# Four attention layers on one core: PSUM laid out by hand (3+3 score banks, one spaced background bank), small units spread singly, masks one tile late

## Chip, cores, metric

One Trainium2 chip, one core. The metric is the device time of one execution in microseconds (us), median of several. A program on one core has one span only. "Granted clock" is the share of TensorE's full clock that the throttle let through.

## The reference, cut

```python
def _A_ref(x, wqkv, wo):              # windowed: key at most 255 behind the query
    qkv = (x @ wqkv).reshape(B, S, 3, H, Dh) ...     # B 1, S 2048, D 640, H 32, Dh 20
    scores = einsum("bhqd,bhkd->bhqk", q, k) * Dh ** -0.5
    mask = (idx[:, None] - idx[None, :] >= 0) & (idx[:, None] - idx[None, :] < 256)
    p = softmax(where(mask, scores, -1e9)); o = einsum("bhqk,bhkd->bhqd", p, v)
    return o.reshape(B, S, D) @ wo
# _B_ref: the same without a mask
x = x + _A_ref(_layernorm(x), A_wqkv, A_wo)   # layer 0
x = x + _B_ref(_layernorm(x), B_wqkv, B_wo)   # layer 1
x = x + _A_ref(_layernorm(x), A_wqkv, A_wo)   # layer 2
x = x + _B_ref(_layernorm(x), B_wqkv, B_wo)   # layer 3
```

## The kernel before

The sequence is cut into four chunks of 512 queries, the heads into eight groups of four. A *unit* is one layer, chunk and head group. A *bank* of scores is 128 keys by 512 queries of one head: 64 banks in a full unit (layers 1 and 3), 12 in a windowed one. Score banks are packed into *tiles*, each one exponential on ScalarE (ACT). TensorE (PE) runs in program order: the scores of a tile, then some *background* work (layer norm transposes, q/k/v projections, output projections, softmax tails), then the products with v of an earlier tile. All order is fixed when the program is built. In the code below, a *tick* is one score tile, and *credit* is the TensorE time, as the program reckons it, that background work may still take after a tile.

```python
psS = pool("psS", 1, PS)   # score tiles: "sa" 3 banks, "sb" 2 banks
psO = pool("psO", 1, PS)   # 1 bank: output of the current unit
psM = pool("psM", 2, PS)   # 2 banks: background
...
def pump(credit):          # background after each score tile, in FIFO order, tails first
    state["credit"] = min(state["credit"] + credit, 1.5)
    while True:
        t = choose(state["credit"] <= 0.0)   # a started matmul group is always finished
        if t is None:
            break
        state["credit"] -= advance(t)

def require(what):         # a demand: run the queue until `what` is there
    while what not in ready:
        t = choose(False)
        if t is None:
            state["tick"] += 1
            continue
        state["credit"] = max(state["credit"] - advance(t), -1.0)
...
# a projection group: five matmuls into one background bank, then an eviction
pq = psM.tile([P, C], F32, name="pq", tag="m")
for dc in range(KD):
    nc.tensor.matmul(pq[:], lhsT=wt[:, n, dc, :], rhs=xt[:, dc, :], ...)
    if dc < KD - 1: yield ("hold", 0.22)
evac(dst, pq[:])           # VectorE; ScalarE in layer 0
...
for c in range(1, NC + 1): # layer 1's chunk c (c = 4: the first part of layer 3) mixed with
    small = deque(Unit(2, c - 1, g) for g in range(G))          # layer 2's windowed units
    for g in range(G if c < NC else SPLIT):                     # SPLIT = 6
        units.append(Unit(1, c, g) if c < NC else Unit(3, 0, g, "a"))
        if g >= 1:
            for _ in range(2):
                if small: units.append(small.popleft())
    units += small
...
for t in ...:              # per tile
    ...                    # demands of a unit that starts here; scores of tile t; its exponential
    ...                    # masks of tile t (VectorE, waits for that exponential)
    pump(1.2 if layer == 0 else 0.43 * n_b + 0.06 - 0.55)       # n_b: banks in the tile
    ...                    # products with v, two tiles late
```

The softmax here doesn't subtract the row's maximum and nothing guards it: scores larger than these inputs give would overflow.

## Time and profile before

| | before |
|---|---|
| time, median of three | 2806.48 us (2802.12 to 2807.31) |
| exponential tiles | 1,946 |
| ScalarE / TensorE / VectorE busy | 82% / 81% / 31% |
| mean granted clock | 0.692 |

ScalarE and TensorE are both four fifths busy, yet neither is full on average: the table by stretch, which the prediction shows, splits the run into stages with ScalarE full and stages with holes.

VectorE (DVE) is the least busy of the three, but its queue stands still for 150 us behind masks that wait for an exponential.

### The profile page before, as it was taken

Reading aid. Unit: us, or ns where it says so; the run is one execution under the profiler, and the core shown is the slowest. Engines: PE = TensorE matmul, PEld = TensorE weight load, DVE = VectorE, ACT = ScalarE, POOL = GpSimd, SP = SyncE. Lnnn points to the kernel's source line nnn. Section 1 sums busy time; section 2 is a strip of 40 time slices with the busy share of each in tenths; the row PEclk is TensorE's granted clock in tenths of the full one; section 3 lists DMA queues with packets and bytes.
Section 4 is the critical chain, followed back from the end, with each engine's and each line's share of the span. In section 5 each row is a group of like instructions: output and inputs, shape, how many; then the busy total and the mean of one; then the engine's idle time right before and its main releaser. Section 6 shows DMA issues by size and latency. Waiting matters only on the chain.

```text
span 2805.3 us, 37851 instructions
## 1 busy us (share of the span) xinstructions
PE 2282.9 (81%) x15325; PEld 753.2 (27%) x15424; DVE 861.1 (31%) x1939; ACT 2298.1 (82%) x2119; POOL 46.6 (2%) x113
## 2 busy tenths in 40 slices
PE   6677777988978898778887788787888888888888
PEld 2233333321322333223332233223221112112112
DVE  5565563320332424233342333433310001001001
ACT  4575663999878888887978788784899999999997
POOL 2000000000000000000000000000000000000000
PEclk8798888985765788557875597757765556556555
DMA  3211002211210133002320032101311001011000
GB/s 129 71 53 39 29 24 71 80 42 51 50 58 15 37 96 88 20 15 59 88 80 16 14 101 63 58 1 47 116 37 45 29 29 53 29 35 48 29 29 10
DMA packets 80799, 139.22 MB, mean 50 GB/s; under 512 B 7536, under 2 KB 49008, under 8 KB 80624
## 3 DMA queue, kind: packets, MB, share of 16 engines
q1 hardware_dynamic: 80624, 136.80, 16.0%
q8 instruction: 120, 1.97, 0.3%
q14 instruction: 55, 0.45, 0.1%
HBM read 107.68 MB, written 29.10 MB: 49 GB/s over the span
## 4 chain that ended last, share of the span: by engine, by line
ACT 31%; PE 17%; issue 8%; DVE 3%; DMA 1%; SPq 0%; ACTq 0%; POOLq 0%; POOL 0%
ACT pt L776 31%; PE pq L275 4%; PE yp L454 3%; PE op L812 3%; PE sa L761 2%; PE sb L761 2%; DVE pt L791 1%; PE pv L354 1%; DMA qt<-q_d 1%; DMA wqk<-wqk_d 0%; PE trp L324 0%; DVE oT L641 0%; PE zb L682 0%; PE rp L675 0%; DVE rz L667 0%
## 5 line engine op out<-in xcount | busy, mean ns | idle before, releaser
L776 ACT ACTIVATE pt<-sa 128x1536 bf16<-128x1536 f32 (+3 forms) x993 | 1421.9, 1434 | 148.8 <-PE sa L761 126.1
L776 ACT ACTIVATE pt<-sb 128x1024 bf16<-128x1024 f32 (+2 forms) x983 | 1008.4, 1027 | 236.7 <-PE sb L761 219.2
L761 PE MATMUL sa<-qt,kt 32*128 32x512 bf16 x2458 | 447.8, 523 | 206.8 <-ACT pt L776 193.9
L812 PE MATMUL op<-pt,vt 128*21 128x512 bf16 x4096 | 552.1, 528 | 13.5 <-DMA vt<-v_d 6.1
L761 PE MATMUL sb<-qt,kt 32*128 32x512 bf16 x1638 | 441.8, 526 | 48.8 <-ACT pt L776 40.6
L761 PEld LDWEIGHTS <-kt 32*128 32x128 bf16 x4096 | 202.0, 96 | 850.4 <-issue 828.9
L275 PE MATMUL pq<-xnT,wqk 128*128 128x512 bf16 x1181 | 368.8, 442 | 51.2 <-DMA wqk<-wqk_d 23.6
L791 DVE TENSOR_TENSOR pt<-pt,masks 128x1024 bf16<-128x1024 bf16 (+5 forms) x422 | 247.7, 610 | 497.1 <-ACT pt L776 495.4
L641 DVE CAST oT<-op 128x512 bf16<-128x512 f32 x122 | 83.5, 685 | 666.2 <-PE op L812 666.2
L812 PEld LDWEIGHTS <-vt 128*21 128x21 bf16 x4096 | 105.9, 92 | 372.3 <-issue 362.9
L454 PE MATMUL yp<-wop,on 128*128 128x320 bf16 x1024 | 184.1, 335 | 3.9 <-DVE on L686 1.4
L275 PEld LDWEIGHTS <-wqk 128*128 128x128 bf16 x1280 | 121.9, 108 | 226.4 <-issue 131.3
L812 PE MATMUL op<-pt,va 128*21 128x384 bf16 (+2 forms) x1408 | 91.4, 335 | 53.3 <-DVE oT L641 47.6
L354 PE MATMUL pv<-wv,xnT 128*128 128x320 bf16 x640 | 119.3, 335 | 7.4 <-DVE vs L236 2.4
L454 PEld LDWEIGHTS <-on 128*128 128x128 bf16 x1024 | 102.6, 108 | 72.3 <-issue 25.2
L236 DVE CAST st<-pq 128x512 bf16<-128x512 f32 x86 | 59.5, 692 | 158.1 <-PE pq L275 154.3
L686 DVE TENSOR_TENSOR on<-oT,zb 128x512 bf16<-128x512 bf16 x128 | 87.6, 684 | 63.7 <-PE zb L682 63.6
L462 DVE TENSOR_TENSOR x_sb<-x_sb,yp 128x320 bf16<-128x320 bf16 x128 | 61.6, 482 | 137.6 <-PE yp L454 137.6
L682 PE MATMUL zb<-rT,spread 32*128 32x128 bf16 x512 | 66.0, 266 | 35.5 <-DVE rT L677 33.4
L761 PE MATMUL sa<-qa,ka 32*128 32x384 bf16 (+2 forms) x846 | 80.7, 337 | 16.7 <-ACT pt L776 15.8
L761 PE MATMUL sb<-qa,ka 32*128 32x384 bf16 (+2 forms) x562 | 76.4, 337 | 4.4 <-ACT pt L776 4.3
L354 PEld LDWEIGHTS <-xnT 128*128 128x128 bf16 x640 | 64.2, 108 | 48.8 <-issue 19.4
(57 smaller groups left out, 780.2 us busy)
## 6 DMA issues: line engine op xcount, KB each, us to landing
wqk<-wqk_d SPq DMA_DIRECT2D x99, 320.0 KB
kt<-k_d SPq DMA_DIRECT2D x50, 512.0 KB
vt<-v_d SPq DMA_DIRECT2D x58, 336.0 KB
qt<-q_d SPq DMA_DIRECT2D x62, 128.0 KB
q_d<-st SPq DMA_DIRECT2D x56, 128.0 KB
v_d<-vs SPq DMA_DIRECT2D x16, 336.0 KB
wqk_d<-wqk SPq DMA_DIRECT2D x16, 320.0 KB
k_d<-kt SPq DMA_DIRECT2D x8, 512.0 KB
```

The source lines that it names most:

```text
L236: nc.vector.tensor_copy(out=out_, in_=in_)
L275: nc.tensor.matmul(pq[:], lhsT=wt[:, n, dc, :], rhs=xt[:, dc, :], start=(dc == 0), stop=(dc == KD - 1),)
L354: nc.tensor.matmul(pv[:], lhsT=xt[:, dc, i * P : (i + 1) * P], rhs=wv_sb[l % 2][:, dc, h * HD : (h + 1) * HD], start=(dc == 0), stop=(dc = ...
L454: nc.tensor.matmul(yp[:], lhsT=on[:, g, qb * P : (qb + 1) * P], rhs=wop[:, g, i * HD : (i + 1) * HD], start=(g == 0), stop=(g == G - 1),)
L462: nc.vector.tensor_tensor(out=xv, in0=xv, in1=yp[:], op=ALU.add)
L641: nc.vector.tensor_copy(out=oT[:], in_=op[:])
L682: nc.tensor.matmul(zb[:, qb * P : (qb + 1) * P], lhsT=spread4[:, qb, :], rhs=rT[:], start=True, stop=True,)
L686: nc.vector.tensor_tensor(out=on[:, g, :], in0=oT[:], in1=zb[:], op=ALU.mult)
L761: nc.tensor.matmul(sp[:, i, col * P : (col + qn) * P], lhsT=u.k(kc, j), rhs=u.q(j, q0, qn), start=True, stop=True,)
L776: nc.scalar.activation(out=pt[:, i:k, b0 * P :], in_=sp[:, i:k, b0 * P :], func=ACT.Exp, scale=SCALE,)
L791: nc.vector.tensor_tensor(out=pt[:, i:k, b0 * P :], in0=pt[:, i:k, b0 * P :], in1=mv_, op=ALU.mult,)
L812: nc.tensor.matmul(op[32 * j : 32 * j + VW, q0 * P : (q0 + qn) * P], lhsT=u.v(kc, j), rhs=pt[:, i, col * P : (col + qn) * P], start=(first ...
```

## The change

Its intent: fewer and larger exponentials (3+3 banks after layer 0 instead of 3+2), a background bank that is never taken again in the tile in which it was filled, so that TensorE does not meet an eviction; masks that do not block VectorE's queue; windowed units spread out; weights fetched ahead.

```diff
-    psS = pool("psS", 1, PS); psO = pool("psO", 1, PS); psM = pool("psM", 2, PS)
+    ps = psp.tile([P, 8, C], F32, name="ps", tag="ps")   # by hand: 0-2, 3-5 scores, 5 and 6
+    op = ps[:, 7, :]                                      # background in layer 0, then 6 alone
...
-        state["credit"] = min(state["credit"] + credit, 1.5)
+        state["credit"] = min(state["credit"] + credit, 1.0)
...
+    def take_m():
+        while True:
+            b = min(mfree, key=mfree.get)
+            if mfree[b][0] <= state["tick"]:
+                mfree[b] = (1 << 30, 0)
+                return b
+            yield ("wait", 1)
+    def drop_m(b):                      # after layer 0 free again only in the next tile
+        mseq[0] += 1
+        mfree[b] = (state["tick"] + (not state["early"]), mseq[0])
+    def end_early():
+        ...
+        del mfree[5]
+        state["early"] = False
...
+            if not order[i][3]:
+                yield ("wait", 4)       # weights: asked for four tiles ahead, one list per layer
...
-        for g in range(G if c < NC else SPLIT):
+        for g in range(G):
             units.append(Unit(1, c, g) if c < NC else Unit(3, 0, g, "a"))
-            if g >= 1: ... two small units
+            for _ in range(((0, 1, 1, 1, 1, 2, 2, 0) if c < NC else (0, 0, 2, 2, 2, 2, 0, 0))[g]):
+                units.append(small.popleft())
...
-            size = 3 if len(tiles) % 2 == 0 else 2
+            size = 2 if len(tiles) % 2 and banks[n][0].l == 0 else 3
...
-                pump(1.2 if cur[0][0].l == 0 else 0.43 * n_b + 0.06 - 0.55)
+                pump(1.2 if cur[0][0].l == 0 else 0.5)
+            # masks of tile t - 1 here, after the background
...
-            if len(pts) >= 4 and pts[3][0] <= t - PV_LAG:
+            if len(pts) >= 4 and pts[3][0] <= t - (3 if pts[0][3][0].windowed else 2):
```

Left out: more buffers (probabilities 3+3 to 6, weights 3 to 4), a cap on values in staging, destinations made only when a group ends.

More of the change, by code (lines that the diff above doesn't have):

```diff
@@ L27 @@
 VW = DH + 1
-PV_LAG = 2
-SPLIT = 6
 @with_exitstack
@@ L52 @@
     big = pool("big", 1)
-    wqkp = pool("wqkp", 3)
+    wqkp = pool("wqkp", 4)
     kvp = pool("kvp", 3)
@@ L60 @@
     onp = pool("onp", 2)
-    ptp = pool("ptp", 3)
+    ptp = pool("ptp", 6)
     otp = pool("otp", 3)
@@ L66 @@
     lnp = pool("lnp", 4)
-    rzp = pool("rzp", 2)
+    rzp = pool("rzp", 3)
     PS = bass.MemoryType.PSUM
-    psS = pool("psS", 1, PS)
-    psO = pool("psO", 1, PS)
-    psM = pool("psM", 2, PS)
+    psp = pool("psp", 1, PS)
     dram = pool("dram", 1, bass.MemoryType.DRAM)
@@ L88 @@
     masks = big.tile([P, 3, C], BF16, name="masks", tag="masks")
-    op = psO.tile([P, C], F32, name="op", tag="o")
+    ps = psp.tile([P, 8, C], F32, name="ps", tag="ps")
+    op = ps[:, 7, :]
     wqk_d = [dram.tile([G, P, 2 * KD * P], BF16, name=f"wqk_d{w}", tag=f"wqk_d{w}") for w in range(2)]
@@ L120, in other_constants @@
         load_wop(0)
-        nc.vector.memset(op[:], 0.0)
+        nc.vector.memset(op, 0.0)
         nc.vector.tensor_copy(
@@ L202, in pump @@
             state["credit"] -= advance(t)
+    mfree = {5: (0, 0), 6: (0, 1)}
+    mseq = [1]
+    def take_m():
[9 more added lines that the diff above has]
+    def end_early():
+        while mfree[5][0] == 1 << 30:
+            advance(state["held"])
+        del mfree[5]
+        state["early"] = False
     def require(what):
@@ L216 @@
     live = Counter()
-    cap = {"qa": 3, "ka": 18, "va": 10, "xnT": 5, "kt": 3, "vt": 3, "qt": 4, "ln": 1}
+    cap = {"qa": 3, "ka": 18, "va": 10, "xnT": 5, "kt": 3, "vt": 3, "qt": 4, "ln": 1, "w": 2, "vs": 2}
     def room(*tags):
@@ L239 @@
     wtiles = {}
-    worder = []
+    worder = {0: [], 1: [], 2: [], 3: []}
     def get_w(w, g, first):
@@ L256, in get_w, with push_proj, take_w, staged @@
         return t
-    def push_proj(key, w, g, gen, first=False):
-        worder.append((key, w, g, first))
+    def push_proj(key, l, w, g, gen, first=False):
+        worder[l].append((key, w, g, first))
         push(key, gen)
-    def take_w(key):
-        i = next(n for n, e in enumerate(worder) if e[0] == key)
+    def take_w(key, l):
+        yield from room("w")
+        order = worder[l]
+        i = next(n for n, e in enumerate(order) if e[0] == key)
         if key not in wtiles:
-            wtiles[key] = get_w(*worder[i][1:])
-        worder.pop(i)
+            wtiles[key] = get_w(*order[i][1:])
+            if not order[i][3]:
+                yield ("wait", 4)
+        i = next(n for n, e in enumerate(order) if e[0] == key)
+        order.pop(i)
         wt = wtiles.pop(key)
-        if i < len(worder) and not wtiles:
-            wtiles[worder[i][0]] = get_w(*worder[i][1:])
-        return wt
+        if i < len(order) and not any(e[0] in wtiles for e in order):
+            wtiles[order[i][0]] = get_w(*order[i][1:])
+        return wt
+    staging = []
+    def staged():
+        t = stp.tile([P, C], BF16, name="st", tag="st")
+        staging.append(t[:])
+        return t[:]
     def project(wt, n, xt, dst):
-        pq = psM.tile([P, C], F32, name="pq", tag="m")
+        mb = yield from take_m()
+        pq = ps[:, mb, :]
         for dc in range(KD):
             nc.tensor.matmul(
-                pq[:], lhsT=wt[:, n, dc, :], rhs=xt[:, dc, :],
+                pq, lhsT=wt[:, n, dc, :], rhs=xt[:, dc, :],
                 start=(dc == 0), stop=(dc == KD - 1),
@@ L280, in project @@
                 yield ("hold", 0.22)
-        evac(dst, pq[:])
+        evac(dst(), pq)
+        drop_m(mb)
         yield ("pe", 0.22)
@@ L321, in t_ln @@
             yield ("wait", 1)
-            trp = psM.tile([P, KD, P], BF16, name="trp", tag="m")
+            mb = yield from take_m()
+            trp = ps[:, mb, :].bitcast(BF16)[:, 0 : KD * P].rearrange("p (c m) -> p c m", c=KD)
             for dc in range(KD):
@@ L326, in t_ln @@
                 )
-            evac(xt[:, :, i * P : (i + 1) * P], trp[:])
+            evac(xt[:, :, i * P : (i + 1) * P], trp)
+            drop_m(mb)
             yield ("pe", 0.4)
@@ L341, in t_v @@
         vs = {}
+        if not windowed:
+            while live["vs"] + len(halves) > cap["vs"]:
+                yield ("wait", 1)
+            live["vs"] += len(halves)
         for i in range(4):
@@ L351, in t_v @@
                     nc.gpsimd.memset(vv[:, :, DH : DH + 1], 1.0)
-                pv = psM.tile([P, HD], F32, name="pv", tag="m")
+                mb = yield from take_m()
+                pv = ps[:, mb, 0:HD]
                 for dc in range(KD):
                     nc.tensor.matmul(
-                        pv[:], lhsT=xt[:, dc, i * P : (i + 1) * P],
+                        pv, lhsT=xt[:, dc, i * P : (i + 1) * P],
                         rhs=wv_sb[l % 2][:, dc, h * HD : (h + 1) * HD],
@@ L363, in t_v @@
                         va[c, i][:, 16 * h : 16 * h + 16, 0:DH],
-                        pv[:].rearrange("p (h e) -> p h e", h=16),
+                        pv.rearrange("p (h e) -> p h e", h=16),
                     )
@@ L368, in t_v @@
                         vs[h][:, :, i, :].rearrange("p g (j e) -> p g j e", j=4)[:, :, :, 0:DH],
-                        pv[:].rearrange("p (g j e) -> p g j e", g=4, j=4),
+                        pv.rearrange("p (g j e) -> p g j e", g=4, j=4),
                     )
+                drop_m(mb)
                 yield ("pe", 0.14)
@@ L377, in t_v @@
                 )
+                live["vs"] -= 1
             ready.add(("v", l, c, h))
@@ L391, in t_qk_window @@
         yield from room("qa", "ka")
-        wt = take_w(key)
+        wt = yield from take_w(key, l)
         q = qap.tile([P, C], BF16, name="qa", tag="qa")
-        yield from project(wt, 0, xnT[l, c], q[:])
+        yield from project(wt, 0, xnT[l, c], lambda: q[:])
         k = kap.tile([P, C], BF16, name="ka", tag="ka")
-        yield from project(wt, 1, xnT[l, c], k[:])
+        yield from project(wt, 1, xnT[l, c], lambda: k[:])
+        live["w"] -= 1
         qa[c, g], ka[c, g] = q, k
@@ L404, in t_qk_full @@
             yield ("wait", 1)
-        wt = take_w(key)
+        wt = yield from take_w(key, l)
         for n, dst in ((1, k_d[l][:, g, c * C : (c + 1) * C]), (0, q_d[l][:, c, g, :])):
-            s_ = stp.tile([P, C], BF16, name="st", tag="st")
-            yield from project(wt, n, xnT[l, c], s_[:])
-            nc.sync.dma_start(out=dst, in_=s_[:])
+            yield from project(wt, n, xnT[l, c], staged)
+            nc.sync.dma_start(out=dst, in_=staging.pop())
+        live["w"] -= 1
         used(l, c)
@@ L423, in t_qk_first @@
             if wt is None:
-                wt = take_w(key)
+                wt = yield from take_w(key, l)
             if c == 0:
@@ L427, in t_qk_first @@
                 q = qtp.tile([P, C], BF16, name="qt", tag="qt")
-                yield from project(wt, 0, xnT[l, c], q[:])
+                yield from project(wt, 0, xnT[l, c], lambda: q[:])
                 qt[l, 0, g] = q
-            yield from project(wt, 1, xnT[l, c], kt[l, 0, g][:, c * C : (c + 1) * C])
+            yield from project(
+                wt, 1, xnT[l, c], lambda: kt[l, 0, g][:, c * C : (c + 1) * C]
+            )
             ready.add(("qk", l, c, g))
@@ L435, in t_qk_first @@
             if c > 0:
-                s_ = stp.tile([P, C], BF16, name="st", tag="st")
-                yield from project(wt, 0, xnT[l, c], s_[:])
-                nc.sync.dma_start(out=q_d[l][:, c, g, :], in_=s_[:])
+                yield from project(wt, 0, xnT[l, c], staged)
+                nc.sync.dma_start(out=q_d[l][:, c, g, :], in_=staging.pop())
                 ready.add(("q", l, c, g))
             used(l, c)
+        live["w"] -= 1
     ons = {}
@@ L451, in t_out @@
             for i in range(2):
-                yp = psM.tile([P, HD], F32, name="yp", tag="m")
+                mb = yield from take_m()
+                yp = ps[:, mb, 0:HD]
                 for g in range(G):
                     nc.tensor.matmul(
-                        yp[:], lhsT=on[:, g, qb * P : (qb + 1) * P],
+                        yp, lhsT=on[:, g, qb * P : (qb + 1) * P],
                         rhs=wop[:, g, i * HD : (i + 1) * HD],
@@ L461, in t_out @@
                 xv = x_sb[:, 4 * c + qb, i * HD : (i + 1) * HD]
-                nc.vector.tensor_tensor(out=xv, in0=xv, in1=yp[:], op=ALU.add)
+                nc.vector.tensor_tensor(out=xv, in0=xv, in1=yp, op=ALU.add)
+                drop_m(mb)
                 yield ("pe", 0.14)
@@ L480, in push_layer @@
             key = ("qk1", c, 0)
-            push_proj(key, 1, 0, t_qk_first(key, 0, [c]))
+            push_proj(key, l, 1, 0, t_qk_first(key, 0, [c]))
             return
@@ L486, in push_layer @@
             if l == 3:
-                push_proj(key, 1, g, t_qk_full(key, l, c, g))
+                push_proj(key, l, 1, g, t_qk_full(key, l, c, g))
             else:
-                push_proj(key, 0, g, t_qk_window(key, l, c, g), first=(l == 0 and c == 0))
+                push_proj(key, l, 0, g, t_qk_window(key, l, c, g), first=(l == 0 and c == 0))
     class Unit:
@@ L542 @@
         small = deque(Unit(2, c - 1, g) for g in range(G))
-        for g in range(G if c < NC else SPLIT):
+        for g in range(G):
             units.append(Unit(1, c, g) if c < NC else Unit(3, 0, g, "a"))
-            if g >= 1:
-                for _ in range(2):
-                    if small:
-                        units.append(small.popleft())
-        units += small
-    units += [Unit(3, 0, g, "b" if g < SPLIT else None) for g in range(G)]
+            for _ in range(((0, 1, 1, 1, 1, 2, 2, 0) if c < NC else (0, 0, 2, 2, 2, 2, 0, 0))[g]):
+                units.append(small.popleft())
+    units += [Unit(3, 0, g, "b") for g in range(G)]
     units += [Unit(3, c, g) for c in range(1, NC) for g in range(G)]
@@ L624, in finish_unit @@
             if not part_o:
-                part_o["t"] = big.tile([P, SPLIT, C], F32, name="raw_o", tag="early_late")
+                part_o["t"] = big.tile([P, G, C], F32, name="raw_o", tag="early_late")
             raw_o = part_o["t"]
-            nc.vector.tensor_copy(out=raw_o[:, g, :], in_=op[:])
+            nc.vector.tensor_copy(out=raw_o[:, g, :], in_=op)
             return
@@ L638, in finish_unit @@
         if u.part == "b":
-            nc.vector.tensor_tensor(out=oT[:], in0=part_o["t"][:, g, :], in1=op[:], op=ALU.add)
+            nc.vector.tensor_tensor(out=oT[:], in0=part_o["t"][:, g, :], in1=op, op=ALU.add)
         else:
-            nc.vector.tensor_copy(out=oT[:], in_=op[:])
+            nc.vector.tensor_copy(out=oT[:], in_=op)
         push_tail(("tail", l, c, g), t_tail(l, c, g, on, oT))
@@ L659, in t_tail @@
         yield ("wait", 2)
-        zp = psM.tile([P, 16], F32, name="zp", tag="m")
+        mb = yield from take_m()
+        zp = ps[:, mb, 0:16]
         for qb in range(4):
@@ L666, in t_tail @@
         rz = rzp.tile([P, 16], F32, name="rz", tag="rz")
-        nc.vector.reciprocal(out=rz[:], in_=zp[:])
+        nc.vector.reciprocal(out=rz[:], in_=zp)
+        drop_m(mb)
         hl = rzp.tile([P, 2, 16], BF16, name="hl", tag="hl")
@@ L673, in t_tail @@
         yield ("wait", 1)
-        rp = psM.tile([32, P], BF16, name="rp", tag="m")
-        nc.tensor.transpose(out=rp[:], in_=hl[:].rearrange("p n r -> p (n r)"), identity=ident[:])
+        mb = yield from take_m()
+        rp = ps[0:32, mb, :].bitcast(BF16)[:, 0:P]
+        nc.tensor.transpose(out=rp, in_=hl[:].rearrange("p n r -> p (n r)"), identity=ident[:])
         rT = rzp.tile([32, P], BF16, name="rT", tag="rT")
-        nc.vector.tensor_copy(out=rT[:], in_=rp[:])
+        nc.vector.tensor_copy(out=rT[:], in_=rp)
+        drop_m(mb)
         yield ("pe", 0.1)
         yield ("wait", 1)
-        zb = psM.tile([P, C], F32, name="zb", tag="m")
+        mb = yield from take_m()
+        zb = ps[:, mb, :]
         for qb in range(4):
@@ L685, in t_tail @@
             )
-        nc.vector.tensor_tensor(out=on[:, g, :], in0=oT[:], in1=zb[:], op=ALU.mult)
+        nc.vector.tensor_tensor(out=on[:, g, :], in0=oT[:], in1=zb, op=ALU.mult)
+        drop_m(mb)
         yield ("pe", 0.3)
@@ L695, in t_tail @@
                     key = ("qk1", "all", gg)
-                    push_proj(key, 1, gg, t_qk_first(key, gg, list(range(NC))))
+                    push_proj(key, 1, 1, gg, t_qk_first(key, gg, list(range(NC))))
                     if gg == 3:
@@ L735 @@
         pushed = set()
-        for t in range(len(tiles) + PV_LAG + 6):
+        for t in range(len(tiles) + 8):
             state["tick"] += 1
@@ L752 @@
                         if u.l == 1 and u.c == 0 and u.g == 0:
-                            state["early"] = False
+                            end_early()
                         start_unit(u)
                     before_bank(b)
-                tag = "sa" if t % 2 == 0 else "sb"
-                sp = psS.tile([P, 3 if t % 2 == 0 else 2, C], F32, name=tag, tag=tag)
+                sp = ps[:, 0:3, :] if t % 2 == 0 else ps[:, 3:6, :]
                 for n in range(2):
@@ L767 @@
                         s_emitted(b[0])
-                width = 3 if t % 2 == 0 else 2
-                pt = ptp.tile([P, width, C], BF16, name="pt", tag=f"pt{width}")
+                pt = ptp.tile([P, 3, C], BF16, name="pt", tag="pt")
                 i = 0
@@ L780 @@
                     i = k
+                for i, b in enumerate(cur):
+                    pts.append((t, pt, i, b))
+                pump(1.2 if cur[0][0].l == 0 else 0.5)
+            else:
+                pump(2.0)
+            if 0 < t <= len(tiles):
+                cur_, pt_ = masked
                 i = 0
-                while i < n_b:
-                    m, b0 = cur[i][2:4]
+                while i < len(cur_):
+                    m, b0 = cur_[i][2:4]
                     k = i
-                    while k < n_b and cur[k][2] == m:
+                    while k < len(cur_) and cur_[k][2] == m:
                         k += 1
@@ L791 @@
                         nc.vector.tensor_tensor(
-                            out=pt[:, i:k, b0 * P :], in0=pt[:, i:k, b0 * P :], in1=mv_,
+                            out=pt_[:, i:k, b0 * P :], in0=pt_[:, i:k, b0 * P :], in1=mv_,
                             op=ALU.mult,
@@ L795 @@
                     i = k
-                for i, b in enumerate(cur):
-                    pts.append((t, pt, i, b))
             if n_b:
-                pump(1.2 if cur[0][0].l == 0 else 0.43 * n_b + 0.06 - 0.55)
-            else:
-                pump(2.0)
-            if len(pts) >= 4 and pts[3][0] <= t - PV_LAG:
+                masked = (cur, pt)
+            if len(pts) >= 4 and pts[3][0] <= t - (3 if pts[0][3][0].windowed else 2):
                 group = [pts.popleft() for _ in range(4)]
```

## The prediction

> **What bounds the kernel now.** I read the busy table by stretch first, cut where the program changes stage. Columns: stretch, its length, then busy time of TensorE, its weight loads, VectorE, ScalarE and GpSimd (count of instructions), granted TensorE clock, DMA share, GB/s.
>
> ```profile
> 47.00:424.00 377.00, 278.40 (x2407) 119.32 (x2436) 217.09 (x521) 232.71 (x280) 13.86 (x32) 0.83 0.13 42
> 424.00:466.00 42.00, 28.92 (x178) 17.78 (x178) 19.78 (x49) 0.63 (x2) 2.96 (x7) 0.78 0.27 77
> 466.00:705.00 239.00, 213.26 (x1339) 64.98 (x1356) 57.08 (x104) 225.41 (x197) 0.00 (x0) 0.81 0.17 59
> 705.00:1926.00 1221.00, 1013.70 (x7035) 344.92 (x7075) 432.41 (x946) 1015.97 (x903) 12.74 (x36) 0.70 0.17 49
> 1926.00:1958.00 32.00, 16.67 (x82) 8.18 (x79) 10.55 (x23) 1.10 (x2) 1.82 (x4) 0.70 0.35 97
> 1958.00:2086.00 128.00, 107.81 (x638) 31.02 (x640) 28.38 (x65) 111.08 (x97) 0.00 (x0) 0.65 0.23 73
> 2086.00:2790.00 704.00, 588.22 (x3431) 147.71 (x3432) 62.77 (x166) 690.10 (x608) 0.00 (x0) 0.54 0.11 35
> ```
>
> These are: layer 0 (windowed); a hole before layer 1; first chunk of layer 1; layers 1 and 2 mixed with the first part of layer 3; a second hole; the rest of layer 3's first chunk; its other three chunks. ScalarE's exponentials bound the last (690 of 704 us) and the third (225 of 239). Elsewhere ScalarE idles: 144 us in layer 0, 41 and 31 in the holes, 205 in the mixed stage.
>
> Next the order in time. The pace with nothing in the way (start, length, engine, operation):
>
> ```profile
> 1138.91 1.49 ACT L776 ACTIVATE pt<-sa 128x1536 bf16<-128x1536 f32 x1
> 1140.26 1.06 ACT L776 ACTIVATE pt<-sb 128x1024 bf16<-128x1024 f32 x1
> 1141.17 1.49 ACT L776 ACTIVATE pt<-sa 128x1536 bf16<-128x1536 f32 x1
> ```
>
> Five score banks take 2.26 us although the two records sum to 2.55: neighbours overlap. And a stall:
>
> ```profile
> 1170.06 4.05 PE L275 MATMUL pq<-xnT,wqk 128*128 128x512 bf16 x9 [0.24 <-issue]
> 1175.01 1.45 ACT L776 ACTIVATE pt<-sa 128x1536 bf16<-128x1536 f32 x1 [4.32 <-PE sa L761]
> 1930.48 0.49 DVE L236 COPY xnT<-trp 128x640 bf16<-128x640 bf16 x1 [0.81 <-PE trp L324]
> 1935.19 7.60 PE L354 MATMUL pv<-wv,xnT 128*128 128x320 bf16 x40
> 1957.29 1.02 ACT L776 ACTIVATE pt<-sb 128x1024 bf16<-128x1024 f32 x1 [30.90 <-PE sb L761]
> ```
>
> Two projection groups stand between two score tiles in TensorE's order because the next unit demanded its q and k at once; at the slow clock they cost ScalarE 4.32 us. The hole at 1926 is the same at length: one demand put an output group, four transpose groups, eight value groups and two projections into one gap. So what decides is how much background stands between neighbouring score tiles.
>
> **What the Trainium skill says.** "ScalarE: Activation LUTs", section "What ACT_TABLE_LOAD costs": an ACTIVATE with immediate scale takes 186 ns + 0.833 ns per column, neighbours overlapping by about 93. The records agree on length (1473 and 1045 ns for 1536 and 1024 columns; the formula gives 1466 and 1039). The overlap is larger here: 690.10 us over 307.2 pairs (1536 banks, five to a pair) is 2.246 a pair, so 57 ns a piece above the columns. "Perfetto Trace Analysis", section "Matmuls": rotate groups through different PSUM banks, so that evacuation overlaps the next group. The trace agrees: with two banks the value groups above follow each other without a gap, while the transposes, held by their input, run one per 1.65 us. "TensorE: Matmul & The Clock Gate", section "What's actually happening": the default state is throttled and activity releases it. Here five projection matmuls take 2.29 us at clock 0.5 and 1.25 at 1.0, and the long waits at 1926 dropped it. "PSUM — Partial Sum Buffer", section "PSUM bank collisions raise a hardware error": two engines must not be on one bank together. So one background bank means matmuls, then eviction, then matmuls.
>
> **The change part by part.**
>
> *3+3 score banks.* 4,864 banks of scores come in 1,946 tiles before and 1,647 after; the difference, 299, times 57 ns is 17 us, spread over the stages after layer 0. A pair of tiles now gives TensorE 2.67 us instead of 2.25, which should spare part of the small stalls.
>
> *Masks one tile late, six probability buffers, windowed value products three tiles late.* A mask no longer stands in VectorE's queue ahead of a background eviction, waiting for the exponential of its own tile (495 us of such waits). Masks cost the same, 248 us. VectorE is not a bound, so this only spares stalls.
>
> *Background budget.* Per tile the credit was 0.80 or 0.37, so 0.234 per bank; it becomes 0.5 per three banks, 0.167, a cut of 29%. After layer 0 there is one bank for background, free again only in the next tile. In normal running that spaces groups well: a projection at the fast clock (1.25 us) fits a 1.34 us tile. But a demand runs whole queues at once, and there the single bank serialises. The compiled order of the changed kernel, which can be read without running it, shows it. Gaps between score tiles in the mixed stage: before, 17 gaps of two projections (4.5 us of idle each by the two that I looked at, 76 us), eight of two output groups (4.1 us, 33) and seven of a transpose and two value groups (3.4 us, 24), together 133, and no longer one until the 1926 hole. After, one gap of two projections, two of 29 groups each (nine projections, eight outputs, four transposes, eight values), two of 16 and one of 11. They stand where the first windowed unit of a chunk, or a unit of layer 3, needs work that waits behind the former chunk's in the queue. The gap before layer 1 grows from 28 groups plus a normalisation tail to 48: 20 projections join it.
>
> Cost of a group in such a gap with one bank: its matmuls, 0.05 us to VectorE, the eviction (0.69 us for 512 columns, 0.49 for 320), 0.05 back. Projection 2.05 us fast, 3.05 slow; output 1.86 or 2.8; value 1.45 or 2.0; transpose 1.65 as now. The 29-group gap: seven fast projections 14.4, eight outputs 15, layer-norm lead 4, transposes 6.6, values 11.6 to 16, two projections 4 to 6; 56 to 62, less 2.5 that ScalarE has in stock: 57 each, 114 for two. The 16-group gaps: one as the 1926 hole (31) plus 0.6 for each of eight values and the rest, 38, the other without reloads of k and q, 33: 71. The 11-group one 27. Before layer 1: 18 projections 37 to 55, the rest about 65, so near 105 instead of 42.
>
> *Unit order.* Eight instead of six units of layer 3 start early, and the last windowed unit ends two units ahead of the part that needs chunk 3. The 1926 hole thus shrinks to 27, but the windowed units of chunk 3 cause 33 of the 71.
>
> *Weights fetched by layer, four ticks ahead.* In layer 0 TensorE waits several times about 5 us for weights; these should go, and the 5 us pairs of projections too.
>
> Sum by stage (before, then after; estimates from the numbers above):
> - start and layer 0: 424, 395 (weight waits about 20, the rest pairs)
> - gap before layer 1: 42, 105
> - first chunk of layer 1: 239, 235 (171 tiles at 1.337 plus 6)
> - mixed stage: 1221 for 2,207 banks; after for 2,304 (two more early units): 768 tiles at 1.337 is 1026, gaps 114 + 71 + 3 = 188, partial tiles 12, small stalls 42 (before 205 - 133 = 72): 1268
> - second hole and rest of that chunk: 160 for 223 banks; after, 126 banks 56, hole 27, waits for k and q that come too late to prefetch 20: 103
> - last three chunks: 704, 694 (512 tiles at 1.337 plus 10)
> - end: 16, 22 (output groups on one bank)
> Together 2806 before, 2822 after. I predict 2820 us.
>
> **Rivals.** (1) It wins clearly: were the mixed stage freed of stalls, the sum would lose 188 and half of the small stalls and come to about 2610. For it speaks the longer tile pair and the free VectorE queue; against it, six long gaps that stand in the program order and that no timing can reorder. If the gaps run at fast clock throughout and small stalls vanish, 2740. (2) The gaps run slow: with one bank TensorE is busy 60 to 70% in them, and after the layer-norm lead it may never see a busy enough stretch to speed up. All groups at the slow clock make the gaps about 75 us dearer: 2890. Against: in layer 0 it stays at 1.0 at 75% busy. (3) The gain is only that of ScalarE's 299 fixed parts, the gaps being work that must be done anyway: 2789. Against: ScalarE idles throughout a gap, and the hole at 1926 shows that.
>
> **Range and chances.** The gaps carry about 320 us, uncertain by 50; layer 0 by 20; small stalls by 30. In 8 of 10 cases 2735 to 2890. That puts most of the chance within 2%, with slower a little likelier than faster by the sum; but such a change is usually kept because it helped, which lifts faster to about the same.
>
> **What would show it.** Right: 1,647 tiles; exponentials of three banks 1.34 us apart in the last stage (694 us); two ScalarE idles of 50 to 60 us in the mixed stage, two of 30 to 40, one near 100 before layer 1, and inside them matmuls that wait for VectorE each time. Wrong: idles half as long (evictions hidden after all), layer 0 below 370 us, or small stalls of over 80 us in the mixed stage because a cold TensorE cannot do a projection within a tile.

## More of the kernel before

All that is queued behind a mask that waits for an exponential waits too, and so does TensorE where it needs it: its own waits for VectorE in layer 0, for two steps of the softmax tails (idle time after the last bar):

```profile
L682 PE MATMUL zb<-rT,spread 32*128 32x128 bf16 x124 | 13.7, 238 | 19.5 <-DVE rT L677 17.4 <-ACT ka L234 1.4 <-ACT pt L776 0.6
L675 PE MATMUL rp<-ident,hl 128*32 128x128 bf16 x31 | 7.3, 236 | 16.8 <-DVE hl L671 13.3 <-ACT pt L776 3.4
```

VectorE's groups in layer 0 of the kernel before (columns: line, engine, operation, tiles, shapes, count | busy us, mean ns | idle time of the engine just before them, and what ended it):

```profile
L791 DVE TENSOR_TENSOR pt<-pt,masks 128x1024 bf16<-128x1024 bf16 (+6 forms) x199 | 117.6, 613 | 151.0 <-ACT pt L776 150.4
```

## The result, and the profile after

2830.3 us (2826.37 to 2837.19, four runs) against 2806.08 (2802.12 to 2807.31, four runs). Ratios are the mean time of one kernel's runs over that of the other's of the same rounds, so not quite the ratio of these medians: 1.0091, interval 1.0069 to 1.0114. So the change costs 0.9%: measurable, but small.

The busy table by stretch of the changed kernel, cut at its own stage ends and with the same columns as in the prediction:

```profile
47.00:327.00 280.00, 242.97 (x2390) 109.22 (x2391) 210.01 (x510) 224.00 (x271) 15.15 (x31) 0.92 0.17 55
327.00:450.00 123.00, 81.43 (x279) 32.94 (x278) 33.92 (x69) 0.20 (x1) 2.35 (x5) 0.58 0.18 53
450.00:697.00 247.00, 202.69 (x1288) 61.80 (x1289) 45.00 (x86) 225.84 (x167) 0.00 (x0) 0.73 0.13 44
697.00:1989.00 1292.00, 1012.60 (x7266) 354.99 (x7263) 432.75 (x941) 1032.76 (x784) 14.59 (x40) 0.71 0.17 49
1989.00:2012.00 23.00, 13.11 (x53) 6.11 (x53) 5.34 (x10) 0.35 (x1) 0.00 (x0) 0.72 0.18 57
2012.00:2107.00 95.00, 66.24 (x377) 20.02 (x376) 23.58 (x52) 57.73 (x42) 0.00 (x0) 0.70 0.26 80
2107.00:2802.00 695.00, 548.33 (x3497) 159.44 (x3496) 65.90 (x173) 689.07 (x514) 0.00 (x0) 0.55 0.11 36
```

Little moved in total because much moved in both directions:

| stage | before | predicted | after |
|---|---|---|---|
| start and layer 0 | 424 | 395 | 327 |
| gap before layer 1 | 42 | 105 | 123 |
| first chunk of layer 1 | 239 | 235 | 247 |
| mixed stage | 1221 | 1268 | 1292 |
| second hole and rest of that chunk | 160 | 103 | 118 |
| last three chunks | 704 | 694 | 695 |
| end | 16 | 22 | 26 |

(The cuts are read to about 2 us. The mixed stage holds 2,208 banks before, counted from the units, 2,304 after; the prediction has 2,207.) The long holes in ScalarE's timeline, from the changed kernel (start, length, engine, operation, count, idle time before and what ended it):

```profile
450.04 4.14 ACT L825 ACTIVATE pt<-ps 128x1536 bf16<-128x1536 f32 x3 [122.83 <-PE ps L811]
1107.40 4.13 ACT L825 ACTIVATE pt<-ps 128x1536 bf16<-128x1536 f32 x3 [60.23 <-PE ps L811]
1455.91 12.20 ACT L825 ACTIVATE pt<-ps 128x1536 bf16<-128x1536 f32 x9 [53.91 <-PE ps L811]
1724.52 4.13 ACT L825 ACTIVATE pt<-ps 128x1536 bf16<-128x1536 f32 x3 [39.04 <-PE ps L811]
1823.12 4.13 ACT L825 ACTIVATE pt<-ps 128x1536 bf16<-128x1536 f32 x3 [28.65 <-PE ps L811]
2012.36 4.14 ACT L825 ACTIVATE pt<-ps 128x1536 bf16<-128x1536 f32 x3 [23.00 <-PE ps L811]
```

Six holes, 328 us together, where the kernel before had two of 41 and 31. What stands in one of them, from the timeline of the changed kernel (matmul groups on PE, evictions on DVE, in brackets the idle time before each and its releaser):

```profile
1055.93 1.24 PE L308 MATMUL ps<-xnT,wqk 128*128 128x512 bf16 x5 [0.78 <-DVE st L256]
1057.21 0.69 DVE L256 CAST st<-ps 128x512 bf16<-128x512 f32 x1 [1.33 <-PE ps L308]
1057.95 1.24 PE L308 MATMUL ps<-xnT,wqk 128*128 128x512 bf16 x5 [0.78 <-DVE st L256]
...
1086.12 1.49 PE L395 MATMUL ps<-wv,xnT 128*128 128x320 bf16 x5 [0.58 <-DVE va L256]
1087.66 0.49 DVE L256 CAST va<-ps 128x320 bf16<-128x320 f32 x1 [1.58 <-PE ps L395]
1088.20 1.49 PE L395 MATMUL ps<-wv,xnT 128*128 128x320 bf16 x5 [0.58 <-DVE va L256]
```

PE and DVE take turns: matmuls, eviction, matmuls. A fast projection costs 2.02 us (1055.93 to 1057.95), 0.78 of it waiting for the bank. A value group costs 2.08, slow. In layer 0, on the other hand, VectorE's masks no longer wait:

```profile
L848 DVE TENSOR_TENSOR pt<-pt,masks 128x1024 bf16<-128x1024 bf16 (+5 forms) x196 | 112.8, 608 | 0.5 <-ACT pt L825 0.5
```

The work is the same (113 us of masks), the idle time before it falls from 151 to 0.5 us. TensorE's waits for VectorE in the two steps shown before are gone too:

```profile
L732 PE MATMUL ps<-rT,spread 32*128 32x128 bf16 x120 | 12.2, 223 | 0.7 <-DVE rT L725 0.3 <-ACT xnT L254 0.2
L723 PE MATMUL ps<-ident,hl 128*32 128x128 bf16 x30 | 7.1, 235 | 1.7 <-DVE hl L718 1.7
```

The granted clock rose with it: layer 0 ran at 0.92 instead of 0.83, and TensorE's busy time there fell from 278 to 243 us for the same work. So faster matmuls can be part of the 97 us, beside fewer waits; the late mask alone brings both (0.91 and 249 us in its own run below), and how they divide was not separated.

### The profile page after: what moved, and what is told of

Read it like the earlier page. It is cut to its first block, busy times and chain, and to the rows that moved or that the text cites. A ratio compares the mean times of both kernels' runs of the same rounds, so it can differ in the third digit from the quotient of the medians. Undisturbed runs are those within 1.5% of the kernel's fastest.

```text
span 2827.8 us, 37330 instructions
## 1 busy us (share of the span) xinstructions
PE 2211.2 (78%) x15424; PEld 766.3 (27%) x15424; DVE 854.7 (30%) x1925; ACT 2257.2 (80%) x1818; POOL 48.5 (2%) x113
## 4 chain that ended last, share of the span: by engine, by line
ACT 46%; PE 29%; issue 13%; DVE 11%; DMA 2%; SPq 0%; POOL 0%; ACTq 0%; DVEq 0%
ACT pt L825 45%; PE ps L308 11%; PE ps L811 5%; PE ps L395 4%; PE ps L501 3%; PE ps L865 3%; DVE pt L848 2%; PE ps L359 1%; DVE x_sb L509 1%; DMA qt<-q_d 1%; DVE st L256 1%; DVE xn L350 1%; DVE vs L256 1%; DVE oT L686 1%; PE ps L732 1%
## 5 line engine op out<-in xcount | busy, mean ns | idle before, releaser
L825 ACT ACTIVATE pt<-ps 128x1536 bf16<-128x1536 f32 (+1 forms) x1678 | 2192.7, 1564 | 506.2 <-PE ps L811 493.4
L811 PE MATMUL ps<-qt,kt 32*128 32x512 bf16 x4096 | 743.0, 523 | 359.1 <-ACT pt L825 316.1
L865 PE MATMUL ps<-pt,vt 128*21 128x512 bf16 x4096 | 554.7, 528 | 12.2 <-DMA vt<-v_d 6.3
L308 PE MATMUL ps<-xnT,wqk 128*128 128x512 bf16 x1280 | 410.7, 463 | 39.7 <-DVE st L256 15.1
L686 DVE CAST oT<-ps 128x512 bf16<-128x512 f32 x120 | 82.3, 686 | 509.1 <-PE ps L865 508.9
L501 PE MATMUL ps<-wop,on 128*128 128x320 bf16 x1024 | 175.5, 318 | 26.0 <-DVE x_sb L509 17.7
L811 PE MATMUL ps<-qa,ka 32*128 32x384 bf16 (+2 forms) x1408 | 141.7, 333 | 47.4 <-ACT pt L825 42.9
L395 PE MATMUL ps<-wv,xnT 128*128 128x320 bf16 x640 | 137.5, 362 | 35.9 <-DVE vs L256 17.4
L736 DVE TENSOR_TENSOR on<-oT,ps 128x512 bf16<-128x512 bf16 x128 | 87.7, 686 | 115.9 <-PE ps L732 114.5
L865 PE MATMUL ps<-pt,va 128*21 128x384 bf16 (+2 forms) x1408 | 90.2, 326 | 14.8 <-DVE oT L686 14.7
```

The lines of the kernel that those rows point to most:

```text
L308: nc.tensor.matmul(pq, lhsT=wt[:, n, dc, :], rhs=xt[:, dc, :], start=(dc == 0), stop=(dc == KD - 1),)
L395: nc.tensor.matmul(pv, lhsT=xt[:, dc, i * P : (i + 1) * P], rhs=wv_sb[l % 2][:, dc, h * HD : (h + 1) * HD], start=(dc == 0), stop=(dc == K ...
L501: nc.tensor.matmul(yp, lhsT=on[:, g, qb * P : (qb + 1) * P], rhs=wop[:, g, i * HD : (i + 1) * HD], start=(g == 0), stop=(g == G - 1),)
L686: nc.vector.tensor_copy(out=oT[:], in_=op)
L736: nc.vector.tensor_tensor(out=on[:, g, :], in0=oT[:], in1=zb, op=ALU.mult)
L811: nc.tensor.matmul(sp[:, i, col * P : (col + qn) * P], lhsT=u.k(kc, j), rhs=u.q(j, q0, qn), start=True, stop=True,)
```

## The experiments

All ten were correct against the reference, and timed in four runs against seven of the kernel before (2805.7 to 2807.1 us). The compiled order of each was read before it ran; the numbers of groups in holes come from there.

**Theory.** Three parts act: (M) the late mask is a large gain; (O) the unit order, helped by a smaller budget, makes the holes; (S) the single bank makes each hole longer. Rivals: the budget alone makes the holes; layer 0's gain comes from the weights.

### Budget alone

```diff
-                pump(1.2 if cur[0][0].l == 0 else 0.5)
+                pump(1.2 if cur[0][0].l == 0 else 0.7)
```

> The changed kernel with the background budget after layer 0 raised from 0.5 to 0.7 a tile, which is the 0.234 a bank of the kernel before. Theory A (the smaller budget makes the holes): the five holes of the mixed stage and after, 205 us together, go, about 2640 us. Theory B (the unit order makes them, the budget only lengthens them): by the compiled order the holes hold 24, 23, 14, 7 and 7 groups instead of 29, 29, 16, 16 and 11; at about 2 us a group they are 152 us, about 2775 us. The gap before layer 1 stays at 123 us in both.

Measured 2767.05 us (2742.94 to 2769.13), ratio 0.984. ScalarE's holes in the profile:

```profile
426.36 2.79 ACT L825 ACTIVATE pt<-ps 128x1536 bf16<-128x1536 f32 x2 [101.30 <-PE ps L811]
1073.72 6.82 ACT L825 ACTIVATE pt<-ps 128x1536 bf16<-128x1536 f32 x5 [44.95 <-PE ps L811]
1413.05 6.82 ACT L825 ACTIVATE pt<-ps 128x1536 bf16<-128x1536 f32 x5 [42.41 <-PE ps L811]
1678.97 1.45 ACT L825 ACTIVATE pt<-ps 128x1536 bf16<-128x1536 f32 x1 [34.88 <-PE ps L811]
```

Together with two of 10.0 and 13.8 the five later holes are 146 us: theory B of the expectation (152). The budget shortens holes and removes none. The profiled run is 2741 us, one of the quicker ones: its gap before layer 1 took 101 us for the same 48 groups, at a mean granted clock of 0.82 instead of 0.58. So the length of this hole went with the clock granted in it, and this kernel scatters by 1%. The 146 us are those of a quick run; the median, 2767, is near theory B's 2775 and far from theory A's 2640.

### Unit order alone

```diff
-            for _ in range(((0, 1, 1, 1, 1, 2, 2, 0) if c < NC else (0, 0, 2, 2, 2, 2, 0, 0))[g]):
+            for _ in range((0, 2, 2, 2, 2, 0, 0, 0)[g]):
```

> The changed kernel with two windowed units after each of units 1 to 4 of a chunk, as before, instead of spread singly. Theory B (order): by the compiled order three holes remain, of 12, 11 and 15 groups, about 82 us instead of 205: about 2710 us. Theory A (budget): the holes stay, 2830. If pairs of windowed units overload VectorE, some 15 us are lost again.

Measured 2671.49 us (2649.14 to 2682.66), ratio 0.9509. Holes of 20.5, 23.0 and 33.2 us are left of the five, 77 us (82 expected), and a new small one of 7.3, beside the gap before layer 1 (122.0). The order alone is worth 159 us on the medians, the budget alone 63. Putting two windowed units in a row did not hurt enough to be seen.

### Order and budget

Both edits. 

> Both: old unit order and 0.7 a tile. By the compiled order one hole of six groups is left after layer 1 begins (about 14 us), and the unchanged gap before layer 1 (123 us). If ScalarE's idle time in a hole is all that holes cost, 2640 us. If the work taken out of the holes comes back as small stalls because TensorE cannot do it beside the scores, over 2720.

Measured 2620.84 us (2598.83 to 2623.65), ratio 0.9321. One hole of 8.6 us is left beside the gap of 120.4. The prediction for this run was 20 us high. So what the holes held can run beside the scores nearly for free, once it is not demanded all at once.

### Masks back behind their own tile

```diff
+                # masks of tile t here, right after its exponential
                 pump(1.2 if cur[0][0].l == 0 else 0.5)
-            # masks of tile t - 1 here
```

> The changed kernel with each mask back right behind the exponential of its own tile. Layer 0 ended at 327 us with late masks and at 424 in the kernel before. Theory M (the late mask made that gain, by freeing VectorE's queue): layer 0 ends at about 390 to 420, and the windowed units of layer 2 lose some 15 us more: about 2910 us. Rival W (the weights fetched ahead and the singly spread projections made it): layer 0 ends below 345, about 2840 us.

Measured 2935.13 us (2915.7 to 2948.81), ratio 1.0435: slower by 105 us than the changed kernel. VectorE's masks in layer 0 and the end of the gap before layer 1:

```profile
L840 DVE TENSOR_TENSOR pt<-pt,masks 128x1024 bf16<-128x1024 bf16 (+6 forms) x199 | 117.6, 613 | 123.8 <-ACT pt L825 123.3
528.38 4.14 ACT L825 ACTIVATE pt<-ps 128x1536 bf16<-128x1536 f32 x3 [122.67 <-PE ps L811]
```

The 124 us of waiting are back, and layer 0 ends at 528.4 - 122.7 = 406 us instead of 327. Theory M holds: 79 of the 97 us that layer 0 gained are the late mask. (The profiled run is the slowest of the four, 2948.81 us; the next experiment gives 81 us by the other way round.) The remaining 18 are those that the weights, the credit cap and the order can have brought; they were not taken apart. The mixed stage grows too, from 1292 to 1336 us.

### Late masks alone, on the kernel before

```diff
-                # masks of tile t, before the background
+            # masks of tile t - 1 here, after the background
-            if len(pts) >= 4 and pts[3][0] <= t - PV_LAG:
+            if len(pts) >= 4 and pts[3][0] <= t - (3 if pts[0][3][0].windowed else 2):
```

> The kernel before with only the masks one tile late (and the value products of windowed units three tiles late). Putting the masks back in the changed kernel moved the end of layer 0 from 327 to 406 us. Theory M (late masks alone give that gain): layer 0 ends near 345 us instead of 424, and the windowed units of layer 2 gain some 10 to 20: about 2715 us. Rival (they only work together with the two other measures, weights ahead and single groups): less than half of it, over 2770.

Measured 2667.94 us (2656.36 to 2669.23), ratio 0.9499: 138 us faster than the kernel before, half as much again as expected. Its stages, same columns as before:

```profile
47.00:343.00 296.00, 248.76 (x2402) 112.32 (x2398) 209.79 (x510) 224.96 (x277) 14.07 (x29) 0.91 0.16 52
343.00:385.00 42.00, 28.36 (x177) 17.89 (x176) 20.28 (x50) 0.65 (x1) 2.97 (x7) 0.78 0.26 69
385.00:624.00 239.00, 214.47 (x1355) 64.74 (x1351) 56.88 (x104) 223.77 (x195) 0.00 (x0) 0.81 0.17 60
624.00:1787.00 1163.00, 1006.95 (x7077) 339.84 (x7075) 426.82 (x945) 1014.07 (x904) 12.75 (x36) 0.72 0.18 52
```

Layer 0 ends at 343 (expected 345), the gap and layer 1's first chunk are as in the kernel before to about 1 us, and the mixed stage takes 1163 instead of 1221: 58 us where I expected 10 to 20. So this one part of the change was worth 138 us on the kernel before, and the others together cost 162, more than all of it.

### Two background banks, 3+2 tiles

```diff
-            size = 2 if len(tiles) % 2 and banks[n][0].l == 0 else 3
+            size = 2 if len(tiles) % 2 else 3
-        del mfree[5]                                  # in end_early
-                pump(1.2 if cur[0][0].l == 0 else 0.5)
+                pump(1.2 if cur[0][0].l == 0 else 0.5 * n_b / 3)
```

> The changed kernel with 3+2 score tiles and two background banks throughout, the background budget per bank of scores left at 0.167, the unit order of the change kept. By the compiled order the holes hold almost the same groups as in the changed kernel (28, 27, 15, 16 and 7 instead of 29, 29, 16, 16 and 11), and the gap before layer 1 holds 25 instead of 48. Theory S (the single bank makes holes longer, each eviction standing between two groups): the 28-group holes take about 38 us instead of 57, the gap before layer 1 about 40 instead of 123; with 17 us for 299 more exponentials about 2720 us. Rival (the second bank does not matter, the groups are bound by TensorE's slow clock): holes as before, about 85 us from the gap before layer 1 alone, 2780.

Measured 2704.0 us (2697.11 to 2718.56), ratio 0.9644. The first four holes:

```profile
362.26 3.71 ACT L822 ACTIVATE pt<-ps 128x1536 bf16<-128x1536 f32 x3 [33.78 <-PE ps L808]
997.27 3.71 ACT L822 ACTIVATE pt<-ps 128x1536 bf16<-128x1536 f32 x3 [35.74 <-PE ps L808]
1334.71 6.89 ACT L822 ACTIVATE pt<-ps 128x1536 bf16<-128x1536 f32 x6 [35.56 <-PE ps L808]
1594.69 3.71 ACT L822 ACTIVATE pt<-ps 128x1536 bf16<-128x1536 f32 x3 [25.39 <-PE ps L808]
```

28 groups take 36 us on two banks, 29 took 54 to 60 on one. Theory S holds: the single bank lengthens a hole by about 20 us in 57. The granted clock does not explain it: it was 0.91 in the changed kernel's hole of 54 us, and 0.90 and 0.86 in these two of 36. The gap before layer 1 falls to a quarter, because it holds fewer groups too.

### Which groups join a demand

With the single bank spaced by tiles, a task that finds it taken steps aside until the next tick, and in a demand the queue passes the turn to whatever is next: 18 projections that nobody asked for joined the gap before layer 1. On top of order and budget:

```diff
+        state["demand"] = True            # at the start of require(), False at its end
-        mfree[b] = (state["tick"] + (not state["early"]), mseq[0])
+        mfree[b] = (state["tick"] + (not state["early"] and not state["demand"]), mseq[0])
```

> Old unit order and 0.7 a tile (2621 us), with one thing more: while a demand is being met, the single bank may be taken again in the same tile. By the compiled order the gap before layer 1 then holds 30 groups instead of 48, the 18 further projections no longer joining; nothing else changes. At about 2.5 us a group in that gap (123 us for 48), 120 becomes about 75: 2575 us. If those projections only come back as work in the first chunk of layer 1, 2600 or more.

Measured 2565.85 us (2562.9 to 2566.4), ratio 0.9141. The gap:

```profile
388.12 2.79 ACT L827 ACTIVATE pt<-ps 128x1536 bf16<-128x1536 f32 x2 [58.87 <-PE ps L813]
```

58.9 us for 30 groups against 120.4 for 48. The gap is 61 us shorter, and 55 of them are gained in the end: done later, beside the scores, the 18 are nearly free. Not all of the 61 is the work of 18 groups, for the granted clock in the gap differs too, 0.84 against 0.62. Against the 48 groups that ran at 0.83 (the 101.3 us of the budget run) it is 42 us, or 2.4 a group; the rest went with the clock.

### Two banks for that gap only

```diff
-            size = 2 if len(tiles) % 2 and banks[n][0].l == 0 else 3
+            size = 2 if len(tiles) % 2 and (banks[n][0].l == 0 or <first unit of layer 1>) else 3
-                        if u.l == 1 and u.c == 0 and u.g == 0:
-                            end_early()
+                        # evictions move to VectorE here; bank 5 is given up one unit later
```

> The same, with two background banks (and 3+2 score tiles) kept until the second unit of layer 1. The gap before layer 1 holds 28 groups against 30 and differs only in having two banks. Theory S (single bank): 28 groups take about 42 us as in the kernel before, not 75: about 2545 us. Rival (TensorE's clock bounds the gap, not the bank): within 10 us of the one-bank version.

Measured 2541.11 us (2538.02 to 2545.91), ratio 0.9058, the fastest version here.

```profile
368.64 2.37 ACT L829 ACTIVATE pt<-ps 128x1536 bf16<-128x1536 f32 x2 [41.13 <-PE ps L815]
```

41.1 us for 28 groups, as the kernel before had (41.4). Between one and two banks lie 18 us, of which two more groups explain about 4. The rival, TensorE's clock, is ruled out by the traces: 0.84 in the gap with one bank, 0.82 with two. The whole run is 25 us faster; where the other 7 us lie was not traced.

### A larger budget still

```diff
-                pump(1.2 if cur[0][0].l == 0 else 0.7)
+                pump(1.2 if cur[0][0].l == 0 else 1.0)
```

> The two-bank-hole version (2541 us) with the budget after layer 0 raised from 0.7 to 1.0 a tile. By the compiled order the hole of six groups at the last part of layer 3's first chunk shrinks to two. If nothing else changes, 6 us: 2535 us. If a tile with a whole group in each is too much for TensorE at its slow clock, small stalls grow and it is over 2555.

Measured 2608.92 us (2603.12 to 2612.33), ratio 0.9293: slower by 68 us, and more so than the warning half of the expectation. No hole grew. What ScalarE waited for TensorE's scores in all (us, times, longest; first the version with 0.7, then 1.0):

```profile
ACT pt L829 <- PE ps L815: 194.4, 211, 41.1
```

```profile
ACT pt L829 <- PE ps L815: 248.8, 288, 40.5
```

77 more stalls, 54 us more. So the budget has an optimum between holes (too little) and small stalls (too much). That a whole group after every tile comes too fast for a TensorE at its slow clock is the likely reason; it was not tested by itself.

### What 3+3 is worth without holes

All of the above (order, demand rule, late masks), but 3+2 tiles and two banks throughout and 0.234 a bank.

> The same order, demand rule and late masks, but 3+2 score tiles and two background banks all through, budget 0.234 a bank: what the 3+3 layout is worth when no hole is in its way. By the compiled order no hole of more than two groups after the gap before layer 1, which stays at 28 groups on two banks. The 299 more exponentials cost 17 us: about 2558 us. Rival 1: the uneven pair of tiles also makes small stalls, over 2580. Rival 2: the second bank saves stalls of its own, below 2541.

Measured 2599.08 us (2598.21 to 2600.0), ratio 0.9261. Against 2541 with 3+3 the uneven layout loses 58 us, which is rival 1.

```profile
ACT pt L824 <- PE ps L810: 221.8, 191, 41.2
```

ScalarE waits 27 us more than the 194.4 above and is busy 26 us more (its busy share over 26 stretches of 100 us is 88.19 against 87.21). The longer busy time is explained in part by the 294 more exponentials in the trace (17 us by the prediction's 57 ns apiece); the other 9 us are not. So 3+3 with one bank beats 3+2 with two once the long holes are gone (tile sizes and banks changed together here); in the change as made the single bank was paid for in six long holes.

## Why the prediction was right, and where not

The total was right (2820 predicted, 2830 measured), and partly by luck: layer 0 ended 68 us below its term, the other stages together came out 74 above theirs, and the two misses cancel.

- *Holes.* Predicted 105 + 188 + 27 = 320 us, measured 122.8 + 181.8 + 23.0 = 328, after four in the mixed stage of 60, 54, 39 and 29 (predicted 57, 57, 38, 33). The mechanism held in detail: matmuls and evictions take turns, at 2.02 us a fast projection (2.05 predicted) and 2.08 a slow value group (2.0). The gap before layer 1 was slow nearly throughout (clock 0.58), hence 18 us more; at 0.82, in the budget run, the same 48 groups took 101.
- *Their cause.* The prediction named where they stand, but told them under the background budget. The runs give the unit order the larger part: the old order alone is worth 159 us, the old budget alone 63. Both together leave one hole of 9.
- *Layer 0: the step that failed.* "VectorE is not a bound, so this only spares stalls" booked the late mask among the small stalls of the mixed stage and gave layer 0 only 29 us, for weights and paired projections. Layer 0 gained 97, so that the prediction's own sign of being wrong, "layer 0 below 370 us", came true; undoing the mask alone takes back 79. The waits for weights that it booked at about 20 us were two, 9.6 us together, in the trace of layer 0 before (PE behind wqk<-wqk_d), and none after. I had the evidence, 495 us of VectorE waiting behind masks, and read a low busy share as proof that its queue could not hold others up. In layer 0 ScalarE evicts the projections, but the softmax tails, the copies of the outputs and the layer norms go through VectorE, and TensorE waits for them: for rT 17.4 us before and 0.3 after, for hl 13.3 and 1.7, for oT 14.4 and 8.9. So a blocked queue can hold the others up at 58% busy (217 of 377 us).
- *Small stalls of the mixed stage.* Predicted to fall from 72 to 42 us. After, 1292 - 1033 = 259 us idle less 182 in holes is 77: nothing gained, if the 72 before are right, which rest on gaps extrapolated from a few. The late mask does spare them: with the masks back behind their own tile they are 110 us (1336 - 1035 idle, less 191 in holes). So something else in the change seems to have added some; which part was not separated.
- *Exponentials.* The last three chunks were predicted at 694 and took 695, so 57 ns per tile spared is right where ScalarE is full.
- *Rivals.* The first, a clear win at 2610, was ruled out by the holes, and rightly for this kernel; with order, budget and demand rule mended, and two banks for the gap before layer 1, the same parts reach 2541, 9.4% below the kernel before.

## What to carry to other kernels

In a program whose order is fixed when it is built, count the work between neighbouring pieces of the bound engine in the compiled order: a demand that runs a queue to its end shows there before anything is run, and a unit moved later can create it. An engine that is a third busy over the run can still set the pace if its queue stands still behind one early-placed wait. When several measures are put in together and the time hardly moves, run each alone: here one was worth 138 us, and the others cost more than that.

## What the Trainium skill lacked or had wrong

- "ScalarE: Activation LUTs" (What ACT_TABLE_LOAD costs): its formula for one ACTIVATE fits (1473 ns measured against 1466), but its 93 ns of overlap between neighbours is too little here. With records of 1.49 and 1.06 us a 3+2 pair repeats every 2.26 us, so about 145 ns overlap, and 57 ns a piece remain above the columns.
- "TensorE: Matmul & The Clock Gate" (What's actually happening): that activity releases the throttle does not say which work counts, only that how busy TensorE has been decides. In the changed kernel TensorE stays at 0.50 while 79% busy, nearly all of it scores and value products (stretch 2200 to 2300), while in layer 0 of the kernel before it stays at 1.00 at 66 to 82% busy (175 to 200 us), where full-width background groups stand among them. That the kind of work makes the difference is not shown. In the gap before layer 1 the same 48 groups ran at 0.58 in one profile and 0.82 in another (122.8 and 101.3 us).
- "Perfetto Trace Analysis" (Matmuls) advises rotating PSUM banks without saying what it costs not to. Here each group on a lone bank waits 0.58 us (320 columns) or 0.78 us (512 columns) for its eviction, and a hole of 28 or 29 groups takes 54 to 60 us on one bank and 36 on two.
- "Perfetto Trace Analysis" (Optimizing Scalar/DVE Operations) says in passing that engines which aren't saturated can cause bubbles on others, and the remedy it names there is to break up instructions; it lacks the one used here, to move a wait later in the queue. VectorE's masks waited 151 us in layer 0 at 58% busy, and moving them one tile back gained 138 us in all.
